# Moving the tiles of an attention and GLU kernel to other byte offsets in SBUF

## The chip, the cores and the metric

The kernel runs on one core of one Trainium2 chip. The metric is the device time of one execution in microseconds (us); the kernel before takes 681.1 us, the median of three runs (680.78 to 681.11).

## The reference

x is 2048 tokens of 448 features. After a layer norm, two branches read the same normalised tokens, and their sum is added to x. The attention branch has 16 heads of 28 features and four segments of 512 tokens; each segment has causal attention of its own and a recall from a running memory of the segments before. The other branch is a gated linear unit with 1792 hidden features. In outline:

```python
xn = layernorm(x)
q, k, v = heads(xn @ wq), heads(xn @ wk), heads(xn @ wv)      # 16 heads of 28
for s in range(4):                                            # segments of 512 tokens
    a_dot = softmax(qs @ ks.T * 28**-0.5 + causal) @ vs
    a_mem = (phi(qs) @ M) / (phi(qs) @ z + 1e-6)
    o = g * a_mem + (1 - g) * a_dot                           # g = sigmoid(beta), a head each
    M += phi(ks).T @ vs;  z += phi(ks).sum(tokens)
attention = concat(o) @ wo
glu = (sigmoid(xn @ w_gate) * (xn @ w_up)) @ w_down
return x + attention + glu
```

All is float32. phi(t) is t + 1 for positive t and exp(t) otherwise.

## The kernel before, in words

**Operands in two halves.** The large products run on float32r operands, and each operand is kept as a high part and a low remainder (`split`, L86). A product is then several matmuls that add up in one PSUM bank. `TERMS` (L52) lists 11 pairs for products over the 448 features: high by high, high by low and low by high of four chunks of features, less one. The down projection has three pairs for each block of 128 hidden features.

**Tiles.** `xs` (L83) holds the normalised tokens, features on the partitions, 7 chunks of 512 tokens for each of four blocks of tokens. `acc` (L84) holds x and takes the results. The pool `mid` (L145) holds 8 KB tiles (`eight_k`: gate-up weights `wgu`, staged weights, the values `vst` and the first half `wo[0]` of the output weights), 4 KB tiles (`four_k`: keys and queries `qk`, and the gated hidden values `hh`), 2 KB tiles and the raw weights from memory. The pool `late` (L158) holds the down weights `wdn`, the weights of the values `wv` and the second half of the output weights. The pool `front` (L276) holds the key and query weights `wqk` and small tiles; later the pool `att` (L626) takes the same space for score operands `qk2`, scores `w` and values `vv`.

**Which operand is which.** A TensorE matmul here has a stationary operand of 128 columns, loaded before it (the profile's PEld rows), and a moving operand whose columns stream through (512 or 448). In the code's `T.matmul(out, stationary, moving)` they are:

| product | line | stationary | moving | columns |
|---|---|---|---|---|
| gate-up (`pgu`) | L246 | `wgu` | `xs` | 512 |
| keys and queries (`pp`) | L344 | `wqk` | `xs` | 512 |
| down (`pd`) | L172 | `hh` | `wdn` | 448 |
| values (`pv`) | L326, L482 | `xs` | `wv` | 448 |
| output (`po`) | L821 | `xs` | `wo` | 448 |
| scores (`st`) | L657 | `qk2` | `qk2` | 512, 384, 256, 128 |
| answers (`pa`) | L732 | `vv` | `w` | 512 to 128 |

**Where tiles lie.** Tiles stand one behind the other in each partition, in the order in which the pools are opened. The allocation puts `xs0` at byte 17024, which is 128 over a multiple of 256. `xs` and `acc` are whole multiples of 256 bytes long (14336 and 7168 a block); `gate` and `gate_n` (L123, L124) take 32 bytes each. So `mid` begins at byte 103104, 192 over a multiple of 256, and since its tiles and those of `late` are whole multiples of 256 bytes too (8192, 4096, 2048, 1792, 3584), `wgu`, `hh`, `wdn`, `wv` and `wqk` all stand at 192. The slices that a matmul takes of a tile (chunks of 512, 1024, 1792 or 2048 bytes) keep this, except that 1792 is an odd multiple of 256.

**Order.** Three stages follow one another, and TensorE's order is written by hand throughout (`manual_schedule`, L276 and L834). The front (L276 to L622) makes the tokens, values, keys and queries of the four blocks and the memory. Then two generators run interleaved from L834: `gated` (L165), the GLU branch, goes through the 14 blocks of hidden features in pairs and for each through the four blocks of tokens; a gate-up group of 11 matmuls yields three times and a down group of 6 twice. `attention` (L745) makes the scores of 32 pairs of heads in five steps each and 16 answers; the main loop (L838 to L848) takes steps of it at the yields, so that score and answer matmuls stand between those of the GLU branch. `project` (L780) makes the output from about 634 us on.

Of the kernel before, what the change touches and what calls it, by code (L numbers as in the profile page):

```python
# [9 lines left out]
F32 = mybir.dt.float32  # L10
# [6 lines left out]
P = 128  # L17
D = 448
# [45 lines left out]
def kernel(  # L64
# [21 lines left out]
    def split(hi, lo, src):  # L86
        A.activation(hi, src, AF.Copy)
        V.tensor_sub(lo, src, hi.bitcast(F32))
# [53 lines left out]
    vd = [dram.tile([P, NT, H * 32], F32, name=f"vd{b}") for b in range(NB)]  # L142
    od = [dram.tile([H * 32, L], F32, name=f"od{b}") for b in range(NB)]

    mid = ctx.enter_context(tc.tile_pool(name="mid", bufs=3, reuse_waits="tile"))  # L145

    def eight_k(dtype, name):
        return mid.tile([P, 8, 256], dtype, name=name, tag="8k")
# [6 lines left out]

    late = ctx.enter_context(tc.tile_pool(name="late", bufs=4, reuse_waits="tile"))  # L158

    def late_pair(name):  # L160
        return late.tile([P, 2, D], F32R, name=name, tag="late")

    rest, begin, wo = [], [], {}

    def gated():  # L165
# [35 lines left out]
        def ready_out(h):  # L201
            if h == 0:
                tile_ = eight_k(F32R, "wo").rearrange("p c n -> p (c n)")
                wo[h] = tile_[:, :2 * D], tile_[:, 2 * D:4 * D]
            else:
                wo[h] = [late_pair("wo").rearrange("p c n -> p (c n)") for _ in range(2)]
            split(*wo[h], raw_up[NF + h][:, :2 * D])
# [10 lines left out]
        for f0 in range(0, NF, FG):  # L218
# [6 lines left out]
            if f0 + FG < NF:  # L225
                ahead[1, 2] = lambda: ready_up(f0 + 2)
                ahead[2, 1] = lambda: (f0 > 0 and ready_down(f0 + 2), load_down(f0 + 3))
                ahead[2, 2] = lambda: load_up(f0 + 4)
                ahead[3, 2] = lambda: ready_up(f0 + 3)
                ahead[3, 3] = lambda: ready_down(f0 + 3)  # L230
                if f0 > 0:
                    ahead[0, 2] = lambda: (load_up(f0 + 3), load_down(f0 + 2))
            else:

                ahead[0, 2] = lambda: load_up(f0 + 3)
                ahead[1, 2] = lambda: ready_out(0)
                ahead[2, 2] = lambda: ready_out(1)
# [38 lines left out]
    with tc.tile_pool(name="front", bufs=2) as sb, tc.manual_schedule(engines=FRONT):  # L276
        stage = eight_k(F32, "stage").rearrange("p (c a) n -> p c (a n)", c=4)
        vst = eight_k(F32, "vst").rearrange("p (t a) (h c) -> p t (a h) c", t=NT, c=32)
        wv = [late_pair("wv") for _ in range(4)]
        wv = [wv[c // 2][:, c % 2, :] for c in range(8)]  # L280
        wqk = {c: sb.tile([P, 8, P], F32R, name=f"wqk{c}", bufs=1) for c in LAST}
        mst = [sb.tile([P, P], F32, name=f"mst{n}", bufs=1) for n in range(2)]
        one = sb.tile([P, 1], F32, name="one", bufs=1)
# [259 lines left out]
        for b in range(NB):  # L543
# [28 lines left out]
            for k, c in enumerate(LAST if last else range(7)):  # L572
# [32 lines left out]
                n = k - 1 if b == 0 else k + 1  # L605
# [20 lines left out]
    sb = ctx.enter_context(tc.tile_pool(name="att", bufs=1, reuse_waits="tile"))  # L626
# [261 lines left out]
```

## Time and profile before

| | |
|---|---|
| time, median of three runs | 681.1 us |
| the profiled execution's own time | 681.4 us |
| its span, first to last instruction | 679.6 us |
| TensorE busy | 675.0 us, 99% |
| weight loads busy | 554.6 us, 82% |
| VectorE busy | 555.9 us, 82% |
| ScalarE busy | 342.5 us, 50% |
| GpSimd busy | 166.2 us, 24% |
| mean granted TensorE clock | 0.999 |

In the profile PE is a matmul on TensorE, PEld a weight load on it, DVE VectorE, ACT ScalarE, POOL GpSimd and SP SyncE. A row of the list of groups gives line, engine, operation, out<-in, shape and count, then the group's busy time in us, the mean duration of one instruction in ns, and the engine's idle time just before it. A row of the timeline gives the start and the length in us of instructions of one kind that stand in a row on one engine, with their count. A row of the windows gives a stretch and its length in us, then busy time and count for PE, PEld, DVE, ACT and POOL, the granted clock, the share of the DMA engines and GB/s. Matmul ends are modelled; their starts are what the rows tell of the pace.

### The profile page before, as it was taken

How to read it: one execution, taken by the hardware profiler on the slowest of the kernel's cores; microseconds unless marked ns; L12 is line 12 of the kernel's file. 1: busy time of each engine (PE TensorE's matmuls, PEld its weight loads, DVE VectorE, ACT ScalarE, POOL GpSimd, SP SyncE). 2: the span in 40 equal slices, each digit the busy share in tenths (PEclk: the TensorE clock that was granted, in tenths of full speed). 3: DMA queues.
4: the chain of work that ended last, by engine and by line, in shares of the span. 5: the costliest groups of instructions: out<-in, count | busy, mean ns of one | idle time of the engine just before them, and what ended most of it. 6: DMA issues, size and time to landing. Idle time of an engine off the chain costs nothing.

```text
span 679.6 us, 11185 instructions
## 1 busy us (share of the span) xinstructions
PE 675.0 (99%) x3963; PEld 554.6 (82%) x3963; DVE 555.9 (82%) x967; ACT 342.5 (50%) x559; POOL 166.2 (24%) x368
## 2 busy tenths in 40 slices
PE   9999999999999999999999999999999999999998
PEld 8888888878878778787877878787787878778897
DVE  6855584758998989998997899988988898989964
ACT  5847573533646446355545545554553655444320
POOL 4402050305122222122322223222231332221000
PEclk9999999999999999999999999999999999999999
DMA  8536768798122242323243334224342332315272
GB/s 270 200 135 247 241 221 268 266 287 220 41 72 86 73 131 68 101 57 103 59 113 83 82 91 101 61 62 108 83 112 73 84 73 68 72 41 130 70 213 99
DMA packets 46223, 84.42 MB, mean 124 GB/s; under 512 B 6360, under 2 KB 21080, under 8 KB 45656
## 3 DMA queue, kind: packets, MB, share of 16 engines
q1 hardware_dynamic: 43160, 76.37, 37.5%
q0 software_dynamic: 3008, 7.34, 5.1%
q8 instruction: 31, 0.51, 0.3%
q14 instruction: 24, 0.20, 0.1%
HBM read 51.05 MB, written 32.64 MB: 123 GB/s over the span
## 4 chain that ended last, share of the span: by engine, by line
PE 99%; POOL 0%; issue 0%; DVE 0%; POOLq 0%
PE pgu L246 43%; PE pd L172 20%; PE pp L344 11%; PE st L657 6%; PE pa L732 5%; PE po L821 5%; PE pv L326 4%; PE pv L482 1%; PE pt L97 1%; PE pk L368 1%; PE warm L463 1%; PE pmm L379 1%; PE n L400 1%; PE warm L466 0%; DVE acc L825 0%
## 5 line engine op out<-in xcount | busy, mean ns | idle before, releaser
L246 PE MATMUL pgu<-xs,wgu 128*128 128x512 f32 x1232 | 319.5, 397 | 0.0
L246 PEld LDWEIGHTS pgu<-xs,wgu 128*128 128x128 f32 x1232 | 226.1, 188 | 47.8 <-issue 2.6
L172 PE MATMUL pd<-wdn,hh 128*128 128x448 f32 x672 | 161.8, 368 | 0.0
L672 POOL TENSOR_SCALAR_AFFINE_SELECT w<-w 128x256 f32<-128x256 f32 (+1 forms) x160 | 76.7, 481 | 247.0 <-ACT w L661 206.2
L172 PEld LDWEIGHTS pd<-wdn,hh 128*128 128x128 f32 x672 | 123.1, 188 | 16.0 <-issue 1.0
L712 ACT ACTIVATE w<-w 128x1024 f32<-128x1024 f32 (+1 forms) x96 | 86.6, 914 | 76.2 <-DVE w L711 75.5
L661 ACT ACTIVATE w<-st 128x512 f32<-128x512 f32 x128 | 75.2, 589 | 56.0 <-PE st L657 52.6
L711 DVE TENSOR_TENSOR w<-w,mb 128x1024 f32<-128x1024 f32 (+1 forms) x96 | 99.6, 1051 | 0.1
L675 DVE TRANSPOSE_TENSOR_REDUCE mx<-w 128x32 f32<-128x1024 f32 x64 | 79.1, 1236 | 14.6 <-POOL w L672 14.6
L344 PE MATMUL pp<-xs,wqk 128*128 128x512 f32 x308 | 77.0, 399 | 0.0
L175 DVE TENSOR_TENSOR acc<-pd,acc 128x448 f32<-128x448 f32 x112 | 67.5, 603 | 2.0 <-PE pd L172 2.0
L344 PEld LDWEIGHTS pp<-xs,wqk 128*128 128x128 f32 x308 | 56.6, 188 | 14.2 <-ACT vst L330 0.8
L657 PE MATMUL st<-qk 84*128 84x128 f32 (+3 forms) x256 | 63.9, 310 | 0.0
L257 ACT ACTIVATE hh<-sg 128x512 fp32r<-128x512 f32 x56 | 35.1, 626 | 42.7 <-DVE sg L256 41.2
L254 ACT ACTIVATE sg<-pgu 128x512 f32<-128x512 f32 x56 | 33.3, 594 | 44.8 <-PE pgu L246 44.7
L657 PEld LDWEIGHTS st<-qk 84*128 84x128 f32 x256 | 48.3, 189 | 8.4
L701 DVE STREAM_TRANSPOSE mb<-top 128x1024 f32<-128x1024 f32 x32 | 39.7, 1240 | 11.0 <-POOL top L698 10.6
L351 DVE TENSOR_TENSOR qk<-pp,qk 128x512 fp32r<-128x512 f32 x28 | 19.4, 692 | 29.8 <-ACT e L349 21.2
L256 DVE SCALAR_TENSOR_TENSOR sg<-sg,pgu 128x512 f32<-128x512 f32 x56 | 37.3, 666 | 5.1 <-PE pgu L246 4.9
L261 DVE SCALAR_TENSOR_TENSOR hh<-sg,hh 128x512 fp32r<-128x512 f32 x56 | 38.6, 689 | 0.6 <-ACT hh L257 0.2
L732 PE MATMUL pa<-w,vv 128*32 128x128 f32 (+3 forms) x512 | 38.2, 436 | 0.0
L821 PE MATMUL po<-wo,xs 128*128 128x448 f32 (+2 forms) x187 | 36.3, 352 | 0.0
(102 smaller groups left out, 619.9 us busy)
## 6 DMA issues: line engine op xcount, KB each, us to landing
qk<-qd SPq DMA_DIRECT2D x192, 112.0 KB
qd<-qk SPq DMA_DIRECT2D x28, 512.0 KB
raw<-in_w_ffn SPq DMA_DIRECT2D x14, 512.0 KB
vd<-vst SPq DMA_DIRECT2D x4, 1024.0 KB
vv<-vd SPq DMA_DIRECT2D x16, 256.0 KB
od<-w POOLq DMA_DIRECT2D x16, 256.0 KB, 4.0
ob<-od SPq DMA_DIRECT2D x32, 128.0 KB
out<-acc SPq DMA_DIRECT2D x15, 224.0 KB
```

The source lines that it names most:

```text
L172: T.matmul(pd[:, :D], l, r, start=n == 0, stop=n == len(mms) - 1)
L175: V.tensor_add(acc[b][:, t, :], pd[:, :D], acc[b][:, t, :])
L246: T.matmul(dst, wgu[f][:, w, side * P:(side + 1) * P], xs[b][:, a, :], start=n == 0, stop=n == len(TERMS) - 1)
L344: T.matmul(pp, wqk[c][:, w, :], xs[b][:, a, :], start=n == 0, stop=n == len(TERMS) - 1)
L657: T.matmul(st[:, at:at + L - kb * P], self.qk[:KS, 1, h, kb * P:(kb + 1) * P], self.qk[:KS, 0, h, kb * P:], start=True, stop=True)
L661: A.activation(w, st, AF.Copy)
L672: G.affine_select(d, d, pattern=pattern, base=0, channel_multiplier=-1, compare_op=ALU.is_ge, fill=MASK)
L675: V.tensor_reduce(mx[:, 16 * (n - 1):16 * (n + 1)], w3[:, n // 2, :2 * L].rearrange("p (b n) -> p b n", n=32), axis=mybir.AxisListType.X, ...
L711: V.tensor_sub(w, w, m)
L712: A.activation(w, w, AF.Exp, scale=SCALE)
L732: T.matmul(pa[32 * j:32 * j + 32, kb * P:], self.vv[:, kb, 32 * j:32 * j + 32], self.pairs[j // 2].block(j % 2, kb), start=kb == 0, stop=k ...
L821: T.matmul(po[:, cols], xs[b][:, a, t * P:(t + 1) * P], out_weights(w)[:, cols], start=m == 0, stop=m == len(TERMS) - 1)
```

## The change

A pad of 48 float32 elements (192 bytes a partition) is put in front of the pool `mid`, one of 16 elements (64 bytes) in front of `late`, and one of 48 elements in front of `wqk` in the pool `front`. No instruction reads or writes a pad. The first half of the output weights is put 16 elements further into its 8 KB tile.

```diff
+    def shift(n, name):
+
+        ctx.enter_context(tc.tile_pool(name=name, bufs=1)).tile([P, n], F32, name=name)
+
+    shift(48, "shift_mid")
     mid = ctx.enter_context(tc.tile_pool(name="mid", bufs=3, reuse_waits="tile"))
...
+    shift(16, "shift_late")
     late = ctx.enter_context(tc.tile_pool(name="late", bufs=4, reuse_waits="tile"))
...
                 tile_ = eight_k(F32R, "wo").rearrange("p c n -> p (c n)")
-                wo[h] = tile_[:, :2 * D], tile_[:, 2 * D:4 * D]
+                wo[h] = tile_[:, 16:16 + 2 * D], tile_[:, 16 + 2 * D:16 + 4 * D]
...
         wv = [wv[c // 2][:, c % 2, :] for c in range(8)]
+        sb.tile([P, 48], F32, name="shift_wqk", bufs=1)
         wqk = {c: sb.tile([P, 8, P], F32R, name=f"wqk{c}", bufs=1) for c in LAST}
```

Over 256 bytes the operands then stand so:

| tile | before | after |
|---|---|---|
| `xs` | 128 | 128 |
| `wgu`, `hh`, `qk`, `vst` and the rest of `mid` | 192 | 128 |
| `wo[0]`, within its tile | 192 | 192 |
| `wdn`, `wv`, `wo[1]` in `late` | 192 | 192 |
| `wqk` and what follows it in `front` | 192 | 128 |
| `qk2`, `vv`, `w` in `att` | 192 | 192 |

## The prediction

> **What bounds the kernel now.** I read the page's shares first, then the chain that ended last, then the windows by stage, and last TensorE alone in order of time.
>
> ```profile
> span 679.6 us, 11185 instructions
> PE 675.0 (99%) x3963; PEld 554.6 (82%) x3963; DVE 555.9 (82%) x967; ACT 342.5 (50%) x559; POOL 166.2 (24%) x368
> PE 99%; POOL 0%; issue 0%; DVE 0%; POOLq 0%
> PE pgu L246 43%; PE pd L172 20%; PE pp L344 11%; PE st L657 6%; PE pa L732 5%; PE po L821 5%; PE pv L326 4%; PE pv L482 1%; PE pt L97 1%; PE pk L368 1%; PE warm L463 1%; PE pmm L379 1%; PE n L400 1%; PE warm L466 0%; DVE acc L825 0%
> ...
> L246 PE MATMUL pgu<-xs,wgu 128*128 128x512 f32 x1232 | 319.5, 397 | 0.0
> L172 PE MATMUL pd<-wdn,hh 128*128 128x448 f32 x672 | 161.8, 368 | 0.0
> ...
> L344 PE MATMUL pp<-xs,wqk 128*128 128x512 f32 x308 | 77.0, 399 | 0.0
> ```
>
> The chain is TensorE from end to end, and the groups that the change touches hold 74% of it: gate-up (1232 matmuls), down (672), keys and queries (308). They have no idle time in front of them. The windows say the same of the stages:
>
> ```profile
> 150.00:300.00 150.00, 150.00 (x781) 122.61 (x780) 137.07 (x227) 76.55 (x121) 41.24 (x101) 1.00 0.36 99
> 300.00:450.00 150.00, 150.00 (x803) 121.59 (x802) 133.13 (x216) 78.52 (x122) 39.17 (x97) 1.00 0.35 86
> 450.00:600.00 150.00, 150.00 (x800) 121.45 (x800) 133.07 (x214) 77.79 (x121) 39.74 (x97) 1.00 0.34 82
> ```
>
> TensorE is busy for all 150 us of each, at the full granted clock (1.00); VectorE comes next with 137.07, 133.13 and 133.07, so TensorE can become some 8% quicker before VectorE is the bound. The program's order on TensorE stays, so the time can change by one thing only: how far apart matmuls that stand in a row start. I call that a slot. A matmul's own duration on the page (397 ns) is modelled and overlaps the next, so I divide the time between the starts of two runs by the count of the first run.
>
> ```profile
> 156.16 0.40 PE L657 MATMUL st<-qk 84*128 84x512 f32 x1
> 156.40 1.79 PE L246 MATMUL pgu<-xs,wgu 128*128 128x512 f32 x7
> 158.03 1.40 PE L172 MATMUL pd<-wdn,hh 128*128 128x448 f32 x6
> 159.26 1.09 PE L246 MATMUL pgu<-xs,wgu 128*128 128x512 f32 x4
> ...
> 162.35 1.38 PE L172 MATMUL pd<-wdn,hh 128*128 128x448 f32 x6
> 163.57 2.72 PE L246 MATMUL pgu<-xs,wgu 128*128 128x512 f32 x11
> 166.14 1.37 PE L172 MATMUL pd<-wdn,hh 128*128 128x448 f32 x6
> 167.35 0.39 PE L657 MATMUL st<-qk 84*128 84x512 f32 x1
> 167.58 2.73 PE L246 MATMUL pgu<-xs,wgu 128*128 128x512 f32 x11
> ```
>
> ```profile
> 642.66 1.40 PE L172 MATMUL pd<-wdn,hh 128*128 128x448 f32 x6
> 643.90 2.37 PE L821 MATMUL po<-wo,xs 128*128 128x448 f32 x11
> 646.10 1.37 PE L172 MATMUL pd<-wdn,hh 128*128 128x448 f32 x6
> 647.31 29.06 PE L821 MATMUL po<-wo,xs 128*128 128x448 f32 x154
> ```
>
> ```profile
> 122.33 2.73 PE L344 MATMUL pp<-xs,wqk 128*128 128x512 f32 x11
> 124.89 1.10 PE L246 MATMUL pgu<-xs,wgu 128*128 128x512 f32 x4
> ```
>
> - Gate-up, 512 columns: (166.14 - 163.57) / 11 = 233.6 ns. Keys and queries, the same shape: (124.89 - 122.33) / 11 = 232.7 ns.
> - Down, 448 columns: runs of six of 1.23, 1.22, 1.21 us, so 3.66 / 18 = 203.3 ns; the two late runs give 206.7 and 201.7.
> - Output, also 448 columns: (646.10 - 643.90) / 11 = 200.0 ns.
>
> While the columns of one matmul stream, the weights of the next are loaded:
>
> ```profile
> 302.88 2.48 PEld L246 LDWEIGHTS pgu<-xs,wgu 128*128 128x128 f32 x11
> 303.07 2.72 PE L246 MATMUL pgu<-xs,wgu 128*128 128x512 f32 x11
> ```
>
> The loads begin one slot ahead of their matmuls, so both operands are read at once. Now put the bytes beside the slots. Over 256 bytes, the streaming operand lies ahead of the operand being loaded by 192 in gate-up and in keys and queries (tokens at 128, weights at 192), by 0 in down (both at 192), by 64 in output and values (weights at 192, tokens at 128). Output and down have the same shape and differ by 3.3 ns. Gate-up has 64 columns more than output and costs 33.6 ns more, yet 64 columns at output's own rate are 64 x 200.0 / 448 = 28.6 ns, 5 ns less. So distance 64 is the cheapest of the three, 192 looks the dearest, 0 lies between. That is what the trace offers in favour of the change; it is a reading of three groups that differ in other things too.
>
> **The change part by part.** It issues nothing: no instruction, DMA or wait is added, removed or moved past another. No queue's order changes. What moves are addresses.
>
> *Down* goes from distance 0 to 64: hh moves back by 64 bytes, wdn stays at 192 (the first pad moves it by 192, the second by 64, together 256). Price: output's 200.0 ns in place of 203.3. How many slots: 672 less those that are followed by a score or answer matmul, whose operands do not move. The code threads 32 x 5 score steps and 16 answer steps between FFN steps, which are 112 x 3 in gate-up and 112 x 2 in down; shared in that proportion, 176 x 0.4 = 70 fall behind a down matmul. 600 x 3.3 = **2.0 us less**. Ends: 0 if 3.3 ns is not of the bytes; 600 x 6.7 = 4.0 us by the late run at 206.7.
>
> *Gate-up and keys and queries* go from 192 to 0. No 512-column matmul over a full array at distance 0 stands in the trace, so I bound it. From below by down at distance 0 plus 64 columns: at most 28.6 ns for these (a slot has a fixed part, so a column costs less than the whole over the columns), at least what two score forms give:
>
> ```profile
> 623.74 0.41 PE L657 MATMUL st<-qk 84*128 84x256 f32 x2
> 623.99 1.79 PE L246 MATMUL pgu<-xs,wgu 128*128 128x512 f32 x7
> ```
>
> A score matmul of 256 columns takes 0.25 / 2 = 0.125 us, one of 512 columns took 0.23 at 167.35: 0.105 us for 256 columns, so 26.2 ns for 64. That makes 229.5 to 231.9 ns; I take the middle, 230.7, and 2.9 ns less than now. Slots: 1540, less 176 x 0.6 = 106 followed by scores or answers, less some 25 keys-and-queries groups followed by a transpose or by the state's matmuls: about 1410. 1410 x 2.9 = **4.1 us less**. The gentler end is output's fixed part, 200.0 + 27 = 227.0 ns: 9.3 us less. The harsh end lies above zero, by the score rows under the rivals.
>
> *Output and values* keep distance 64: wo's first half is put 16 elements into its tile, which undoes the tile's move. Nothing. *Scores*: qk2 moves by 256 and its own slots stay; a score matmul ahead of a gate-up or down matmul goes from 0 to 64, at most 64 slots of 512 columns at 3 ns, 0.2 us, left out. *The other engines* read and write the moved tiles at other bytes; if that cost VectorE some, its cover is the 13 to 17 us of each 150 us in which it is idle while TensorE is not.
>
> Sum, against the profiled execution's 681.4 us (span 679.6): 681.4 - 2.0 - 4.1 = 675.3. The median of the runs is 681.1, 0.3 lower, so I forecast **675.0 us**.
>
> A rule stands against all of this. The Trainium skill, TensorE: Matmul & The Clock Gate, Step-by-step: what each phase is for, says that TensorE has two independent read ports into SBUF, one for the streaming operand and one for the weight load, so that loading the next weights takes nothing from the running matmul. By it addresses would change no slot and the time would stay at 681.1; the 3.3 ns between down and output, at equal shape, speak against it, weakly.
>
> **The rivals.**
>
> *A, the forecast:* distance 0 costs gate-up what it costs down. 675.0.
>
> *B, gate-up falls to output's level,* 227.0 ns: 1410 x 6.6 = 9.3, with down's 2.0: 669.8. For it: down's runs are not one value (201.7 and 206.7 in the rows above), so distance 0 has a good and a bad state, and long gate-up runs might settle in the good one. Against it: down's early six-runs sit near 203, not at 200.
>
> *C, bytes do not matter* (the ports rule above, or the pads not doing what they say): 681.1. For it: down varies by 5 ns at one distance, so something else moves slots too. Against it: output's 200.0 against 203.3, and the 5 ns that gate-up pays beyond its columns. A half of it, *C2*: down gains, gate-up stays: 679.1.
>
> *D, slower: for 512 columns, distance 0 is the worst,* both operands starting on the same bytes. The place is gate-up's and keys-and-queries' 1410 slots. The scores are 512-column matmuls at distance 0 to the weights that follow:
>
> ```profile
> 152.76 0.40 PE L657 MATMUL st<-qk 84*128 84x512 f32 x1
> 153.00 0.86 PE L246 MATMUL pgu<-xs,wgu 128*128 128x512 f32 x3
> ...
> 179.34 0.40 PE L657 MATMUL st<-qk 84*128 84x512 f32 x1
> 179.58 0.78 PE L172 MATMUL pd<-wdn,hh 128*128 128x448 f32 x3
> ```
>
> Their slots are 0.24, 0.24, 0.23 and 0.24 us (152.76, 156.16, 167.35, 179.34), mean 237.5 ns, 3.9 above gate-up: 1410 x 3.9 = 5.5 more, 2.0 less by down, 684.6. It decides from 233.6 + 2.0 us / 1410 = 235.0 ns upward. Against it: stamps are rounded to 10 ns, and a score uses 84 rows with 128-row weights behind it, a switch that gate-up does not have.
>
> **How the numbers follow.** A 0.50, B 0.17, C 0.13, C2 0.06, D 0.14. The likeliest is A, 675.0. The range reaches down past B to 668 (a stamp's rounding is 1 ns a slot over a run of eleven, 1.4 us) and up past C to 682, which leaves out D and little else. A measurement of this kernel can tell about 0.2%, 1.4 us. Faster: A, B and C2, 0.73; same: C, 0.13; slower: D, 0.14.
>
> **What would show it.** Gate-up runs of eleven should last 11 x 230.7 = 2.54 us from start to start (2.57 now; B 2.50, D 2.61); keys and queries likewise; down runs of six 1.20 (1.21 to 1.24 now); output runs of eleven 2.20 as before. TensorE should stay at 99% with the chain unchanged, VectorE's busy time within 1%. Wrong outright would be: a shorter time with unchanged slots (then waits went, not conflicts), or new idle time in front of L246 or L172.

## The result, and the profile after

The changed kernel takes 675.22 us (median of six runs, 674.71 to 675.66) against 681.03 (680.78 to 681.31) in the same session: ratio 0.9915, 95% interval 0.9903 to 0.9928. The forecast was 675.0. The sum was right and its two terms were not: gate-up, keys and queries gave more than forecast and down gave next to nothing, and the two errors cancelled. The groups of the page after say so at once (lines are 6 or 7 further down in the changed file: L252 is L246, L178 is L172, L351 is L344, L828 is L821).

```profile
span 673.4 us, 11185 instructions
PE 668.1 (99%) x3963; PEld 554.1 (82%) x3963; DVE 555.1 (82%) x967; ACT 341.6 (51%) x559; POOL 169.1 (25%) x368
PE 98%; DMA 1%; SPq 0%; ACT 0%; issue 0%; DVE 0%
...
L252 PE MATMUL pgu<-xs,wgu 128*128 128x512 f32 x1232 | 315.0, 394 | 0.0
L178 PE MATMUL pd<-wdn,hh 128*128 128x448 f32 x672 | 161.4, 367 | 0.0
L351 PE MATMUL pp<-xs,wqk 128*128 128x512 f32 x308 | 75.5, 395 | 0.0
```

The same 11185 instructions, the same counts in every group, TensorE still at 99%, VectorE's busy time within 0.8 us. The chain is TensorE's for 98%; its first stretch now goes back to a load of value weights. A group's busy time counts a run of matmuls once from its first start, so its difference is that of the slots: gate-up 319.5 to 315.0, keys and queries 77.0 to 75.5, together 6.0 us; down 161.8 to 161.4, 0.4 us. The span went from 679.6 to 673.4, 6.2 us. TensorE in order of time, at the places shown of before:

```profile
156.10 1.37 PE L178 MATMUL pd<-wdn,hh 128*128 128x448 f32 x6
157.31 1.09 PE L252 MATMUL pgu<-xs,wgu 128*128 128x512 f32 x4
158.23 0.40 PE L664 MATMUL st<-qk 84*128 84x384 f32 x2
...
161.59 2.65 PE L252 MATMUL pgu<-xs,wgu 128*128 128x512 f32 x11
164.08 1.37 PE L178 MATMUL pd<-wdn,hh 128*128 128x448 f32 x6
165.29 0.40 PE L664 MATMUL st<-qk 84*128 84x512 f32 x1
165.53 2.68 PE L252 MATMUL pgu<-xs,wgu 128*128 128x512 f32 x11
168.05 0.40 PE L664 MATMUL st<-qk 84*128 84x384 f32 x2
```

```profile
637.68 2.36 PE L828 MATMUL po<-wo,xs 128*128 128x448 f32 x11
639.88 1.36 PE L178 MATMUL pd<-wdn,hh 128*128 128x448 f32 x6
```

A run of eleven gate-up matmuls now takes 2.49 us (164.08 - 161.59) or 2.52 (168.05 - 165.53), 226.4 and 229.1 ns a slot, where it took 233.6. A run of four takes 0.92 us, 230 ns. Over all 38 runs of eleven, those next to scores and answers included, the mean slot went from 234.7 to 230.3 ns; over the 37 runs of four from 235.6 to 231.6. (Means like these are worked out from the start of every matmul in the two traces.) Two down runs of six take 1.21 us, 201.7 ns against a mean of 203.3; output's eleven take 2.20, as before.

### The profile page after: what moved, and what is told of

Its sections match the earlier page's. It is cut to its first block, busy times and chain, and to the rows that moved or that the text cites. A ratio compares the mean times of both kernels' runs of the same rounds, so it can differ in the third digit from the quotient of the medians.

```text
span 673.4 us, 11185 instructions
## 1 busy us (share of the span) xinstructions
PE 668.1 (99%) x3963; PEld 554.1 (82%) x3963; DVE 555.1 (82%) x967; ACT 341.6 (51%) x559; POOL 169.1 (25%) x368
## 4 chain that ended last, share of the span: by engine, by line
PE 98%; DMA 1%; SPq 0%; ACT 0%; issue 0%; DVE 0%
PE pgu L252 43%; PE pd L178 21%; PE pp L351 11%; PE st L664 6%; PE pa L739 6%; PE po L828 5%; PE pv L333 4%; PE pv L489 1%; PE pt L97 1%; PE pk L375 1%; DMA wv_raw<-in_w_v 1%; PE pmm L386 1%; PE n L407 1%; SPq L427 0%; SPq L424 0%; ACT wv L455 0%
## 5 line engine op out<-in xcount | busy, mean ns | idle before, releaser
L252 PE MATMUL pgu<-xs,wgu 128*128 128x512 f32 x1232 | 315.0, 394 | 0.0
L252 PEld LDWEIGHTS pgu<-xs,wgu 128*128 128x128 f32 x1232 | 226.3, 188 | 44.1 <-issue 2.6
L178 PE MATMUL pd<-wdn,hh 128*128 128x448 f32 x672 | 161.4, 367 | 0.0
L679 POOL TENSOR_SCALAR_AFFINE_SELECT w<-w 128x256 f32<-128x256 f32 (+1 forms) x160 | 80.0, 502 | 236.2 <-ACT w L668 201.7
L178 PEld LDWEIGHTS pd<-wdn,hh 128*128 128x128 f32 x672 | 123.1, 188 | 15.4 <-issue 1.0
L351 PE MATMUL pp<-xs,wqk 128*128 128x512 f32 x308 | 75.5, 395 | 0.0
L351 PEld LDWEIGHTS pp<-xs,wqk 128*128 128x128 f32 x308 | 56.6, 188 | 12.8 <-ACT vst L337 0.8
L828 PE MATMUL po<-wo,xs 128*128 128x448 f32 (+2 forms) x187 | 36.3, 352 | 0.0
```

The costliest lines, as they stand in the source:

```text
L178: T.matmul(pd[:, :D], l, r, start=n == 0, stop=n == len(mms) - 1)
L252: T.matmul(dst, wgu[f][:, w, side * P:(side + 1) * P], xs[b][:, a, :], start=n == 0, stop=n == len(TERMS) - 1)
L351: T.matmul(pp, wqk[c][:, w, :], xs[b][:, a, :], start=n == 0, stop=n == len(TERMS) - 1)
L679: G.affine_select(d, d, pattern=pattern, base=0, channel_multiplier=-1, compare_op=ALU.is_ge, fill=MASK)
L828: T.matmul(po[:, cols], xs[b][:, a, t * P:(t + 1) * P], out_weights(w)[:, cols], start=m == 0, stop=m == len(TERMS) - 1)
```

## The experiments

Three theories were told apart. **A**, of the prediction: a slot is set by how far, over 256 bytes, its moving operand lies ahead of the weights that are loaded at the same time. **C**: bytes do not matter. **S**, formed on seeing down: distance sets the pace that a run settles in, but what stands ahead of the run decides where it starts, and a short run does not get there. Each of the small kernels m1, m2 and m3 below was executed once.

**m1, the distances alone.** Two tiles of numbers, one moving and one stationary, and one run of 33 matmuls for each distance:

```diff
+    def run(name, cols, d, rounds):
+        bank = ps.tile([P, 512], F32, name=name, tag="b", bufs=8)
+        back = (64 - d // 4) % 64
+        for r in range(rounds):
+            for n, (a, w) in enumerate(TERMS):
+                if cols == 512:
+                    m, f = moving[:, 512 * a:512 * a + 512], 256 * w + 128 * (r % 2)
+                else:
+                    m, f = moving[:, D * w:D * w + D], 512 * a + 128 * (r % 4)
+                T.matmul(bank[:, :cols], fixed[:, back + f:back + f + P], m,
+                         start=n == 0, stop=n == len(TERMS) - 1)
```

> All of the reference's arithmetic is left out; x is copied to the output. TensorE alone runs 33 float32r matmuls in a row at each of 16 distances (moving operand ahead of the stationary one by 0, 16, ... 240 bytes over 256), first with 512, then with 448 columns. Theory A (a slot is set by the distance of the two operands that are read at once): with 512 columns about 233 ns at 192, 229 at 0, 227 at 64; with 448 columns 200 at 64 and 203 at 0. Rival C (bytes do not matter): one value for 512 columns and one for 448, within 1 ns, at all distances. Theory S (a run settles in a state by what stood ahead of it): values that differ between distances without order, and slots within one run that are not the same at its start and its end.

TensorE in order of time; the name of a row holds its distance, wide is 512 columns and less is 448:

```profile
29.16 7.64 PE L60 MATMUL wide000b<-moving,fixed 128*128 128x512 f32 x33
36.64 7.65 PE L60 MATMUL wide016b<-moving,fixed 128*128 128x512 f32 x33
44.13 7.87 PE L60 MATMUL wide032b<-moving,fixed 128*128 128x512 f32 x33
51.84 7.82 PE L60 MATMUL wide048b<-moving,fixed 128*128 128x512 f32 x33
59.49 7.73 PE L60 MATMUL wide064b<-moving,fixed 128*128 128x512 f32 x33
67.06 7.75 PE L60 MATMUL wide080b<-moving,fixed 128*128 128x512 f32 x33
...
120.84 7.85 PE L60 MATMUL wide192b<-moving,fixed 128*128 128x512 f32 x33
128.53 7.86 PE L60 MATMUL wide208b<-moving,fixed 128*128 128x512 f32 x33
...
151.62 6.85 PE L60 MATMUL less000b<-moving,fixed 128*128 128x448 f32 x33
158.31 6.87 PE L60 MATMUL less016b<-moving,fixed 128*128 128x448 f32 x33
165.02 6.77 PE L60 MATMUL less032b<-moving,fixed 128*128 128x448 f32 x33
171.62 6.91 PE L60 MATMUL less048b<-moving,fixed 128*128 128x448 f32 x33
178.37 6.77 PE L60 MATMUL less064b<-moving,fixed 128*128 128x448 f32 x33
184.98 6.87 PE L60 MATMUL less080b<-moving,fixed 128*128 128x448 f32 x33
```

Start to start over 33: with 512 columns 7.48 us at 0 (226.7 ns), 7.49 at 16, 7.71 at 32, 7.57 at 64 (229.4), 7.69 at 192 (233.0). With 448 columns 6.69 at 0 (202.7), 6.60 at 32 (200.0), 6.61 at 64 (200.3), 6.75 at 48. This is TensorE alone, no other engine at work, so C is out: at one shape the pace hangs on where the two operands lie. By the rule of two independent read ports in the Trainium skill (TensorE: Matmul & The Clock Gate, Step-by-step: what each phase is for), as the prediction read it, no address would change a slot; 226.7 and 233.0 ns at one shape speak against that reading. It is A's map, with one thing A had wrong: for 512 columns the cheapest distance is 0, not 64. Slots that change along a run, which S in its first form expected, are not seen: at 448 columns and distance 0 the single slots go round about 207, 202, 203, 202 and 199 ns from the start of the run to its end.

**e1, keys and queries alone.** The kernel before with one pad:

```diff
+        sb.tile([P, 48], F32, name="shift_wqk", bufs=1)
         wqk = {c: sb.tile([P, 8, P], F32R, name=f"wqk{c}", bufs=1) for c in LAST}
```

> The kernel before with the pad ahead of the key and query weights alone; all else as before. Theory A: keys and queries lose what the changed kernel's do (73.5 to 72.1 us from start to start), so 1.4 us less, about 679.6. Rival C: 681.0.

679.99 us, ratio 0.9979 (0.9970 to 0.9988). The groups of its page:

```profile
L250 PE MATMUL pgu<-xs,wgu 128*128 128x512 f32 x1232 | 319.6, 397 | 0.0
...
L349 PE MATMUL pp<-xs,wqk 128*128 128x512 f32 x308 | 75.6, 396 | 0.0
```

Only the group whose operand moved changed, 77.0 to 75.6: 1.4 us, as A had it.

**e2, the hidden values alone,** and **e3, the change without them.** The 4 KB tiles get a pool of their own, so that `hh` can be put apart from `wgu`. e2 against the kernel before (e3 is the changed kernel with the same pool, and 16 elements ahead of it in place of those ahead of `late`):

```diff
-        return mid.tile([P, 2, L], dtype, name=name, tag="4k", bufs=4)
+        return four.tile([P, 2, L], dtype, name=name, tag="4k", bufs=4)
...
+    shift(48, "shift_four")
+    four = ctx.enter_context(tc.tile_pool(name="four", bufs=4, reuse_waits="tile"))
+    shift(16, "shift_late")
     late = ctx.enter_context(tc.tile_pool(name="late", bufs=4, reuse_waits="tile"))
```

> The kernel before with the hidden values alone moved back by 64 bytes, so that down goes to distance 64 and gate-up stays at 192. Theory A as the prediction priced it: 600 slots at 3.3 ns, 2.0 us less, 679.0. Theory S (down's slots hang on the run ahead of them, not on their own distance): within 0.5 us of before, 680.5 to 681.5, as in the changed kernel, where down's starts gave only 0.2 us.

> The changed kernel with the hidden values left where they were, so that down stays at distance 0 and gate-up, keys and queries go to 0. Theory A as priced: 2.0 us above the changed kernel, 677.2. Theory S: within 0.5 us of the changed kernel's 675.2.

e2: 681.49 us, ratio 1.0002 (0.9993 to 1.0010). e3: 675.68, ratio 0.9914 (0.9900 to 0.9927). Moving down from 0 to 64 is worth nothing to speak of on either side; A's price of 3.3 ns a slot falls for the kernel's down runs. e2's page has

```profile
L253 PE MATMUL pgu<-xs,wgu 128*128 128x512 f32 x1232 | 319.9, 397 | 0.0
L179 PE MATMUL pd<-wdn,hh 128*128 128x448 f32 x672 | 161.7, 368 | 0.0
```

against 319.5 and 161.8 before: down 0.1 us less, gate-up 0.4 more. The order on TensorE is the same in both kernels, so the runs can be compared one by one. In e2 the 70 down runs of three take 0.53 us longer in all (208.6 to 211.2 ns a slot) and the 73 runs of six 0.52 us less (205.7 to 204.5). The first slot of a run gets 3.3 ns longer on average, the fourth and fifth 3.9 and 3.0 shorter: so the runs of three lose by the move what the runs of six gain.

**e4 and e5, other distances for gate-up.** The weights of gate-up, keys and queries go 64 and 128 bytes lower over 256 than the tokens, the rest stays as in the changed kernel. e4 against the changed kernel (e5 has 16, 32, 48 and 16 in these places):

```diff
-    shift(48, "shift_mid")
+    shift(32, "shift_mid")
...
+    shift(16, "shift_four")
+    four = ctx.enter_context(tc.tile_pool(name="four", bufs=4, reuse_waits="tile"))
...
-                wo[h] = tile_[:, 16:16 + 2 * D], tile_[:, 16 + 2 * D:16 + 4 * D]
+                wo[h] = tile_[:, 32:32 + 2 * D], tile_[:, 32 + 2 * D:32 + 4 * D]
...
-        sb.tile([P, 48], F32, name="shift_wqk", bufs=1)
+        sb.tile([P, 32], F32, name="shift_wqk", bufs=1)
```

> The changed kernel, but with gate-up, key and query weights so that the tokens lie 64 ahead of them in place of 0. Theory A with the map (228.8 ns at 64, 226.7 at 0, 233.4 at 192): 1410 slots lose 2.1 ns of the 6.8, so about 677 to 678, between the changed kernel and before. Rival (any shift of the weights off 192 does it): 675.2.

> The same with the tokens 128 ahead of gate-up, key and query weights. Theory A with the map (233.5 at 128 as at 192): nothing is left of the gain, 681.0 to 681.4. Rival (any shift of the weights off 192 does it): 675.2.

e4: 677.37 us, ratio 0.9943 (0.9925 to 0.9960), where A put it. e5: 679.71, ratio 0.9973 (0.9962 to 0.9983), a little better than A's 681: most of the gain is gone, some 1.5 us is left. So it is not enough to move the weights off 192. Gate-up's group in e4 and e5:

```profile
L254 PE MATMUL pgu<-xs,wgu 128*128 128x512 f32 x1232 | 316.9, 396 | 0.0
```

```profile
L254 PE MATMUL pgu<-xs,wgu 128*128 128x512 f32 x1232 | 318.7, 397 | 0.0
```

With 315.0 at distance 0 and 319.5 at 192 the order is that of the map, 0 before 64 before the rest. Why 128 keeps 0.8 us of it was not tried. The trace shows where it lies: gate-up's second to fifth slots of a run are 231.3, 231.2, 230.7 and 231.3 ns on average against 233.2, 232.9, 233.6 and 233.2 before, the sixth and seventh 234.6 and 235.9 against 233.4 and 232.7.

**e6, everything 64 bytes further.** The changed kernel with one more line ahead of all tiles:

```diff
+    ctx.enter_context(tc.tile_pool(name="shift_all", bufs=1)).tile([P, 16], F32, name="shift_all")
     keep = ctx.enter_context(tc.tile_pool(name="keep", bufs=1))
```

> The changed kernel with one more pad of 64 bytes ahead of everything, so that all tiles lie 64 further over 256 and every distance stays. Theory A: the changed kernel's 675.2 within 0.5. Rival B2 (it is the weights' own byte that counts, 192 bad and 128 good): gate-up weights stand at 192 again, 681.

675.19 us, ratio 0.9907 (0.9889 to 0.9926), with gate-up at 315.0 and down at 161.4 to the digit of the changed kernel's page. Gate-up weights stand at 192 again and cost nothing there: the distance counts, not the byte, as far as this one shift shows.

**m2, runs in the kernel's order.** TensorE alone again, but with gate-up and down interleaved as in one group, at 16 sets of bytes:

```diff
+        wide = [(moving[:, 512 * (a % 4):512 * (a % 4) + 512], 256 * w + wgu // 4) for a, w in TERMS]
+        less = [(moving[:, 2048 + D * w + wdn // 4:][:, :D], 2112 + 512 * a + hh // 4)
+                for _ in range(2) for a, w in ((0, 0), (0, 1), (1, 0))]
+        list_ = [*wide[:4], *less[:3], *wide[4:8], *less[3:], *wide[8:]] * rounds
```

> All of the reference's arithmetic is left out; x is copied to the output. TensorE alone runs the order of one gate-up group with its two pieces of down, 4 + 3 + 4 + 3 + 3 matmuls of 512 and 448 columns, four times in a row (68 matmuls), at 16 sets of bytes; a name such as g064h064d064 says where gate-up weights, hidden values and down weights lie over 256 behind the tokens. Theory A (each slot by its own distance): by the map of the run before, 11 x 233.4 + 6 x 202.7 = 3.78 us a group at g064h064d064, 15.1 us for four; 0.07 us less at g064h000d064; 11 x 226.7 + 6 x 200.1 = 3.69, 14.8 us for four, at g000h000d064; 0.06 us more at g000h064d064. Theory S (short runs do not settle): going over to d064 or h000 alone changes the 68 matmuls by less than 0.03 us, and gate-up's gain is smaller than 11 x 6.7 ns a group.

```profile
28.14 15.28 PE L59 MATMUL g064h064d064b<-moving,fixed 128*128 128x512 f32 x68
43.26 15.34 PE L59 MATMUL g064h000d064b<-moving,fixed 128*128 128x512 f32 x68
58.44 15.20 PE L59 MATMUL g000h064d064b<-moving,fixed 128*128 128x512 f32 x68
73.47 15.17 PE L59 MATMUL g000h000d064b<-moving,fixed 128*128 128x512 f32 x68
88.48 15.19 PE L59 MATMUL g000h000d000b<-moving,fixed 128*128 128x512 f32 x68
...
178.69 14.94 PE L59 MATMUL g000h192d000b<-moving,fixed 128*128 128x512 f32 x68
193.46 15.21 PE L59 MATMUL g000h224d032b<-moving,fixed 128*128 128x512 f32 x68
```

The first four are the bytes of before, e2, e3 and the changed kernel: 15.12, 15.18, 15.03 and 15.01 us from start to start. Going over to distance 64 for down costs 0.06 us in the first pair and gives 0.02 in the second, where A has 24 x 2.4 ns = 0.06 less in both. Gate-up's move gives 0.09 and 0.17 where A has 44 x 6.3 ns = 0.28. So A's sum of single slots does not hold in a mixed order. S is right in kind, a smaller gain than A's in both parts, but not in size: it had less than 0.03 us either way for down, and the first pair changed by 0.06. The best set, g000h192d000, took 14.77.

**e7 and e8, the best set in the kernel.** Hidden values 64 bytes lower than the tokens (192 behind them, in the way m2 counts), down weights level with them; e8 puts the score and answer operands level with the tokens too (it leaves out the last pad). e7 against the changed kernel:

```diff
+    shift(48, "shift_four")
+    four = ctx.enter_context(tc.tile_pool(name="four", bufs=4, reuse_waits="tile"))
     shift(16, "shift_late")
...
-        return late.tile([P, 2, D], F32R, name=name, tag="late")
+        off = 0 if name == "wdn" else 16
+        return late.tile([P, 2 * D + 64], F32R, name=name, tag="late")[:, off:off + 2 * D].rearrange("p (c n) -> p c n", c=2)
...
-        sb.tile([P, 48], F32, name="shift_wqk", bufs=1)
...
+    shift(16, "shift_att")
     sb = ctx.enter_context(tc.tile_pool(name="att", bufs=1, reuse_waits="tile"))
```

> The changed kernel with down's two operands both 64 bytes lower (hidden values 64 behind the tokens, down weights level with the tokens). Down's own distance is still 64 and gate-up's 0; what changes are the distances where one run hands over to the next: tokens to hidden values 0 to 64, down weights to gate-up weights 64 to 0. Theory A (own distance alone): the changed kernel's 675.2. Theory S with the mixed run: four groups took 14.77 us from start to start at these bytes and 15.01 at the changed kernel's, so 28 x 0.24 = 6.7 us less at most, 668.5; with scores and answers in between, somewhere from 669 to 673.

> The kernel of the run before with the score and answer operands 64 bytes lower too, level with the tokens. The scores' own distance stays 0; handing over from gate-up to scores goes from 192 to 0, from scores to gate-up from 64 to 0. Theory A: 675.2. Theory S: below the run before by up to 176 hand-overs and the slots behind them at a few ns, 1 to 2 us.

675.37 us, ratio 0.9913 (0.9900 to 0.9927), and 675.19, ratio 0.9911 (0.9897 to 0.9924): no better than the changed kernel. What S promised from m2 did not carry over. m2 repeats one order four times from one start, without the score matmuls that cut the kernel's runs; its 0.24 us may have been of that order, which was not tried further. The two pages move time between the groups (gate-up 315.4 and 315.8, down 161.2 and 160.8) and the sum stays.

**m3, the length of a run.** Eight stretches of 3 to 11 gate-up matmuls, each followed by a run of 3, 6, 12 or 24 down matmuls:

```diff
+        list_ = []
+        for k in WIDE:
+            list_ += (wide * 2)[:k] + (less * 4)[:length]
```

> All of the reference's arithmetic is left out; x is copied to the output. TensorE alone: eight stretches of 3 to 11 gate-up matmuls (55 in all), each followed by a run of 3, 6, 12 or 24 down matmuls (24, 48, 96, 192 in all); n06g064h000 is runs of six with gate-up weights at 64 and hidden values at 0; down weights at 64 throughout. Question: why moving the hidden values from 64 to 0 gained nothing in the kernel when a long run gains 2.6 ns a matmul. Theory S (a run needs some slots to settle): h000 against h064 gains about 0.4 us or more at 24, 0.2 at 12, and nothing or a loss at 3 and 6. Theory A: 0.06, 0.12, 0.25 and 0.5 us in this order. Rival S2 (with gate-up in between the gain is gone at any length, the state being set at the hand-over): within 0.1 us at all four lengths.

```profile
43.10 17.82 PE L61 MATMUL n03g064h064b<-moving,fixed 128*128 128x512 f32 x79
60.76 17.90 PE L61 MATMUL n03g064h000b<-moving,fixed 128*128 128x512 f32 x79
78.50 17.74 PE L61 MATMUL n03g000h064b<-moving,fixed 128*128 128x512 f32 x79
96.07 17.75 PE L61 MATMUL n03g000h000b<-moving,fixed 128*128 128x512 f32 x79
113.66 22.65 PE L61 MATMUL n06g064h064b<-moving,fixed 128*128 128x512 f32 x103
136.14 22.71 PE L61 MATMUL n06g064h000b<-moving,fixed 128*128 128x512 f32 x103
158.69 22.39 PE L61 MATMUL n06g000h064b<-moving,fixed 128*128 128x512 f32 x103
180.91 22.51 PE L61 MATMUL n06g000h000b<-moving,fixed 128*128 128x512 f32 x103
203.26 32.40 PE L61 MATMUL n12g064h064b<-moving,fixed 128*128 128x512 f32 x151
235.50 32.31 PE L61 MATMUL n12g064h000b<-moving,fixed 128*128 128x512 f32 x151
267.66 32.01 PE L61 MATMUL n12g000h064b<-moving,fixed 128*128 128x512 f32 x151
299.51 32.10 PE L61 MATMUL n12g000h000b<-moving,fixed 128*128 128x512 f32 x151
331.44 52.14 PE L61 MATMUL n24g064h064b<-moving,fixed 128*128 128x512 f32 x247
383.42 51.51 PE L61 MATMUL n24g064h000b<-moving,fixed 128*128 128x512 f32 x247
434.77 51.71 PE L61 MATMUL n24g000h064b<-moving,fixed 128*128 128x512 f32 x247
486.32 51.32 PE L61 MATMUL n24g000h000b<-moving,fixed 128*128 128x512 f32 x247
```

With gate-up at distance 192, h000 against h064, start to start: 17.74 against 17.66 us with runs of three, 22.55 against 22.48 with six, 32.16 against 32.24 with twelve, 51.35 against 51.98 with twenty-four. So the move to distance 64 costs 0.08 and 0.07 us, then gives 0.08 and 0.63. With gate-up at distance 0, as in the changed kernel, it costs 0.02, 0.13 and 0.08 us with runs of three, six and twelve (17.59 against 17.57, 22.35 against 22.22, 31.93 against 31.85) and gives only at twenty-four, 0.39 by the lengths of the last two rows. So long runs gain and short ones do not, but the length at which the sign turns hangs on what stands around the runs; in the kernel it lies between three and six (e2). The amount at twelve is below S's 0.2; rival S2, which has no gain at any length, is out at twenty-four.

The starts of the single matmuls show how. In n06g000h000 a run of eleven gate-up matmuls behind a run of six has slots of 235, 234, 236, 224, 231, 235, 229, 232, 231, 227 and 226 ns, where m1 holds 226 and 227 throughout: this run comes to its pace only near its end. And distance does not fix one pace for each length. With gate-up at 192, five of the eight runs of 24 down matmuls at distance 0 hold 202.3 to 202.5 ns and three hold 206.4; at distance 64 all eight hold 200.4 to 200.8. The gain of 0.63 / 192 = 3.3 ns a matmul is a mean over these two levels, and that it equals the 3.3 ns that the prediction had read from output's runs is chance.

## Why the prediction was right, and where it was not

- **What bounds it.** Right: TensorE throughout, same counts, and the slots account for the span, 6.0 + 0.4 us of busy time in three groups against 6.2 of span.
- **That distance moves slots.** Right, by m1 and e6; the evidence it was read from (3.3 ns between down and output, 5 ns between gate-up and output beyond the columns) was thin but real: at 448 columns m1 has 202.7 at 0 and 200.3 at 64. C is out by m1, and by e4 and e5 beside e6.
- **Down, 2.0 us less.** This step failed. It priced down's 600 slots by output's 200.0 ns; it measured 0.4 us in the group, and by e2 (1.0002) and e3 the move gives nothing. Output runs for eleven and more matmuls in a row and settles; down is cut into threes and sixes. In the changed kernel the runs of three take 0.29 us longer in all than before, those of six 0.72 less and the one run of 24 0.20 longer; in e2 the runs of three and of six cancel. The row of a long run was taken for the price of a short one.
- **Gate-up, keys and queries, 4.1 us less.** Right in kind, too small: 4.5 + 1.5 = 6.0 us. The slot at distance 0 was bounded from down's at distance 0 plus 64 columns, 230.7 ns. m1 has 226.7 at 512 columns against 202.7 at 448, so distances do not rank alike for both lengths: 0 is the best for 512 and not for 448. 226.7 was rival B's level, and the kernel's gate-up comes to it only late in a run: the mean slot went from 233.2 to 231.2 ns at the second place of a run, from 233.2 to 227.3 at the fifth and from 234.1 to 227.2 at the tenth. So 6.0 us over 1410 slots are 4.3 ns, between A's 2.9 and B's 6.6.
- **The sum.** 1.6 too much for down and 1.9 too little for the rest cancelled. That the forecast is within 0.2 us is luck; that the time falls, and by shorter slots alone, was read rightly.
- **Rival D** came out the other way: the score rows that it was built on are single slots between two other kinds, and say no more of a settled pace than down's short runs do. B's reason, a good and a bad state at distance 0, is seen in m3 for runs of 24 with 448 columns.
- **What would show it.** 2.54 us for eleven gate-up matmuls against 2.49 and 2.52; 1.20 for six down matmuls against 1.21; output 2.20 as said; VectorE within 1% as said.

## What to carry to other kernels

Where TensorE is busy from end to end and matmuls of 32-bit operands stand at an even pace, the pace itself can be a cost: divide start-to-start time by the count, compare groups of like shape, and look at where the moving and the stationary operand lie to each other over 256 bytes. Pads that no instruction touches were worth 0.85% here. Price such a change by runs of the length that the kernel has: a pace read from a long run does not hold for runs of three and six, nor does the best set of bytes of one repeated order hold in another.

## What the runs showed of the hardware

- The pace of long runs depends on the distance of the two operands over 256 bytes: with 512 columns 226.7 ns at 0, 227.0 at 16, 229.4 at 64, 230.0 at 80 and 231.8 to 234.5 at the others; with 448 columns 200.0 at 32, 200.3 at 64 and 200.6 at 160, 202.7 at 0, 204.5 at 48 (m1). Steps of 16 bytes matter: 16 and 32 differ by 6.6 ns with 512 columns.
- The effect is TensorE's own, with every other engine idle (m1), and it is the distance that counts: moving all tiles by 64 bytes changed nothing (315.0 and 161.4 us in both).
- A run behind matmuls of another kind does not take its pace at once: gate-up's mean slot in the changed kernel is 231.2 ns at the second place of a run and 227.2 at the tenth.
- One distance can hold two paces: with 448 columns at distance 0 runs of 24 held 202.3 to 202.5 or 206.4 ns (m3). What decides between them was not tried.
